# Attention and gated projection on one core: score blocks of two heads in one scheduled operation, bfloat16 sums over partitions, and new planner numbers

## The chip, the cores and the metric

The kernel runs on one core of one Trainium2 chip. The metric is device time in microseconds (us), the median of the timed runs. In rows, PE is TensorE's matmul, PEld its weight load, DVE is VectorE, ACT is ScalarE, POOL is GpSimd, and SP is the engine whose queue issues the transfers.

## The reference

Causal attention for 4 batches of 12 heads, 448 tokens, head dimension 64, in float32; then its output, as 1792 tokens by 768, goes through a gated product and two projections:

```
scores = scale * q @ k.T;  masked above the diagonal;  attn = softmax(scores)
x   = (attn @ v), heads side by side          # 1792 x 768
a   = x @ w1;  b = x @ w2                     # 768 -> 1024
out = ((a * b) @ w3) @ w_out                  # 1024 -> 1024 -> 768
```

## The kernel before

**Arithmetic.** Large products run on float16 halves: an operand is scaled by a power of two and split into a high and a low float16, and three matmuls (high·high, high·low, low·high) add up in one PSUM bank. The scale comes from a root of the sum of squares: ScalarE squares a tile and sums each row (`squares`), TensorE adds the row sums over all 128 partitions with one matmul by a matrix of ones (`root_scale`, float32, one column), and three small VectorE operations make the power of two and its inverse. The two last weights are multiplied ahead, w3·w_out, in float32 (`w34_mm`, line 738), so that each batch needs a gate (lines 862 to 864) and one projection (lines 922 to 924).

**Attention.** A "pair" is two heads; there are 6 pairs in a batch and 24 in all. Its score blocks are numbered u: 0 to 2 are head one's row blocks of 128, 256 and 384 causal columns, 3 to 5 the same of head two, and 6 is the last 64 rows of both heads together, 448 wide. Head one lies on partitions 0 to 63 and head two on 64 to 127, so the contraction is 64 rows high and the two heads use two halves of the array ("row" below; block 6 uses two quarters, "quad"; the products with v use column halves, "col"). In batches 0 and 1 q and k are float32 (`turned_whole`, each matmul is two records in the trace); in batches 2 and 3 they are float16 halves (`halved`, three matmuls to a block, each one record), and each of q and k has its own `root_scale`. Each block leases one PSUM bank, TensorE writes it (line 535), VectorE scales, masks, takes the row maximum (line 548), ScalarE takes the exponential and its row sum (line 552). `inverse` makes the reciprocals (lines 559, 562), once for blocks 0 to 5 and once for block 6. `soft` makes the float16 halves (lines 577 to 584), a transposing transfer turns them, and `values` multiplies by v (lines 605, 610) into the single "av" bank, which lines 619 and 622 empty into `xt`.

**PSUM.** Eight banks: mm 2, sc 4, tr 1, av 1. The first three row blocks of w3·w_out (`nf=3`, two banks each) hold both mm banks, three of the four sc banks and av while they accumulate over eight steps.

**Order.** Nothing is ordered by hand. Every operation is registered with a due time, its engines with a cost for each, and its reads and writes (`prog.add`). `Program.order` plays a list schedule in Python: on each engine the available operation with the least due time goes first, a bank is leased when the first operation that uses it starts, and instructions are emitted in that order. Due times come from the numbers in `PLAN`. `flex` and `pflex` are added to the due time of an operation that could run on several engines when VectorE or GpSimd considers it. Before, each head's block (and in batches 2 and 3 each of its three products) is an operation of its own that can be parted from its partner by other work.

Of the kernel before, what the change touches and what calls it, by code (L numbers as in the profile page):

```python
# [12 lines left out]
F32 = mybir.dt.float32  # L13
# [13 lines left out]
PLAN = dict(nc=10, wstep=1.7166, soft=35.104, w0=98.515, w34=0.4939, ab=1.864, out=0.1056, gap=7.934, lat=54.674, begin=124.998, wlead=108.279, urgent=16.283, flex=130.436, sc=-28.657, vo=40.18, av=-169.824, x=-3.797, qlead=-32.59, rlead=35.586, v0=19.144, v1=119.702, gram=2, nf=3, h0=3, hv=5, ns=7, wo0=-202.976, wo1=85.211, wom=33.979, w3a=4.552, w3l=33.088, wd=8.804, wh=-51.436, wl=37.619, fin=-41.134, ev=24.84, po=[-24.82, -29.77, -25.56, 9.87, -19.33, -0.94, -43.34, -41.67, -23.49, 5.24, -22.89, 3.16, 5.14, -57.04, -27.78, -11.26, -24.23, -9.57, -25.8, -22.59, -36.97, -12.49, -9.7, 9.83], wo=[-14.34, 44.19, 8.45, 71.74, 57.42, 19.24, 47.18, 16.79], w3=[-59.5, -58.87, -85.5, 5.22, 4.06, -19.4, -19.39, -66.35], tw=[-46.97, -85.5, -45.39, -9.91, -31.02, -57.6, -51.35, -51.53, -46.68, -51.96, -96.47, -10.29, -68.89, -30.15, -61.14, 9.88], slack=0.7, pflex=74.578, fq=2, hlead=23.223)  # L27
# [6 lines left out]
}  # L34

# [11 lines left out]
class Program:  # L47
# [3 lines left out]
    def __init__(self):  # L51
        self.ops, self.writer, self.readers = [], {}, {}
        self.banks, self.leased, self.first = {}, [], set()
# [5 lines left out]
    def add(self, due, how, reads=(), writes=(), stage=None):  # L59
# [17 lines left out]
        self.ops.append((round(due + 3.7e-5, 3), how, deps, stage))  # L77
        leases = [k for k in list(reads) + list(writes) if isinstance(k, Lease)]
        self.leased.append(leases[0] if leases else None)
        if leases:  # L80
            if not leases[0].users:
                self.first.add(i)
            leases[0].users += 1
        return i

    def order(self):
# [12 lines left out]
        dma_free = 0.0  # L99
# [11 lines left out]
        while len(result) < n:  # L111
# [22 lines left out]
            lease = self.leased[i]  # L134
            if i in self.first:
                found = [(at, n_, k) for k in lease.pools for at, n_ in banks[k]]
                if not found:
                    waiting.append(i)
                    continue
                at, n_, k = min(found)  # L140
                if at > t:
                    ready_at[i] = at
                    push(i)
                    continue
                banks[k].remove((at, n_))
                lease.bank, lease.home = self.banks[k][n_], (k, n_)
# [7 lines left out]
            else:  # L154
                if e == DVE and cost > 0.4:
                    cost += 0.4 * max(0.0, min(free[POOL], t + cost) - t)
                if e == PE and cost:
                    if t - free[PE] > 3.4 or not free[PE]:
# [6 lines left out]
            if lease is not None:  # L165
# [36 lines left out]
def tile_causal_attention_moe(ctx: ExitStack, tc: tile.TileContext, q, k, v, w1, w2, w3, wo, out):  # L202
# [47 lines left out]
    ones32 = cst.tile([P, P], F32, name="ones32")  # L250
    diag = cst.tile([P, P], BF16, name="diag")
    nc.vector.memset(ones, 1.0)
    nc.vector.memset(ones32, 1.0)
# [104 lines left out]
    def root_scale(sums, keys, name, due, keep=None):  # L358


        e, ek = keep or small(1, f"{name}_e")
        s, sk = small(1, f"{name}_s")
        ps, pk = prog.lease("sc", "tr")

        def total():
            for j, am in enumerate(sums):
                nc.tensor.matmul(ps[:, 0:1], ones32, am, start=j == 0, stop=j == len(sums) - 1)

        prog.add(due, (PE, 0.05 + 0.15 * len(sums), total), keys, [pk])
        prog.add(due, (DVE, 0.1, lambda: nc.vector.tensor_scalar(  # L370
            out=e.bitcast(I32), in0=ps[:, 0:1].bitcast(I32), scalar1=1, scalar2=0x7F800000,
# [3 lines left out]
        prog.add(due, (DVE, 0.09, lambda: nc.vector.reciprocal(out=s, in_=e)), [ek], [sk])  # L375
        return s, sk, e, ek

    def scaled(dst, src, s, n, due, reads, writes, view=None):
# [7 lines left out]
        ], reads, writes)  # L386

    def remainder(dst, src, s, hi, n, due, reads, writes, stage=None):

        prog.add(due, (DVE, t_dve(n) + 0.06, lambda: nc.vector.scalar_tensor_tensor(  # L390
            out=dst, in0=src, scalar=s, in1=hi, op0=ALU.mult, op1=ALU.subtract)), reads, writes, stage)
# [67 lines left out]
    def halved(p, b, hs, T, qk, qkk, qt, qtk):  # L459

        q16 = qt.rearrange("p i f -> p (i f)").bitcast(F16).rearrange("p (i t f) -> p i t f", i=2, t=2)
        inverse_of = []
        for i, src in ((1, k), (0, q)):
# [9 lines left out]
            am, ak = small(1, "qam")  # L473
            squares(am, flat, lambda n16=n16: n16[:, 1].bitcast(BF16), 4 * P, T - PLAN["hlead"], raw_k, [ak, nk])
            sc_, sck, e, ek = root_scale([am], [ak], "q", T - PLAN["hlead"])
            inverse_of.append((e, ek))
            scaled(n16[:, 0], flat, sc_, 4 * P, T - PLAN["hlead"] + 0.5, raw_k + [sck], [nk])
            remainder(n16[:, 1], flat, sc_, n16[:, 0], 4 * P, T - PLAN["hlead"] + 1, raw_k + [sck, nk], [nk])
# [3 lines left out]
        (ek_, kk), (eq_, kq) = inverse_of  # L482
        prog.add(T, (DVE, 0.1, lambda: nc.vector.tensor_scalar(  # L483
            out=iv, in0=ek_, scalar1=eq_, scalar2=-SCALE, op0=ALU.mult, op1=ALU.mult)), [kk, kq], [ivk])
# [8 lines left out]
    def pair(p):  # L493
# [28 lines left out]
        def scores(u, due):  # L522
            i, c, w, lo = place(u)
            ps, key = prog.lease("sc")
            (t32, tk) = heads[i]
            o = t32[:, lo : lo + w]
            m = mask_t if i == 2 else mask[:, (2 - c) * P :]

            n = min(P, S - c * P)

            def products(qs, ks, start, stop):
                for j in range(2):
                    rows = slice(j * D, (j + 1) * D)
                    if i in (2, j):
                        nc.tensor.matmul(ps[rows if i == 2 else slice(0, P), :w], qs[rows, c * P : c * P + n], ks[rows, 0:w],  # L535
                                         start=start, stop=stop)

            if halves:
                q16 = qt.rearrange("p i f -> p (i f)").bitcast(F16).rearrange("p (i t f) -> p i t f", i=2, t=2)
                for m_, (a, b_) in enumerate(((0, 0), (0, 1), (1, 0))):  # L540
                    prog.add(due + 0.01 * m_, (PE, t_mm(w) / (1 if i == 2 else 2) + 0.02, lambda a=a, b_=b_, m_=m_: products(
                        q16[:, 0, a], q16[:, 1, b_], m_ == 0, m_ == 2)),
                        [qtk + (1,), qtk + (0,)], [key, tk + (c,)] + ([tk] if p < 2 else []))
            else:
                prog.add(due, (PE, 0.9 if i == 2 else max(2 * t_mm(w) + 0.1, 0.31), lambda: products(
                    qt[:, 0], qt[:, 1], True, True)),
                    [qtk + (1,), qtk + (0,)], [key, tk + (c,)] + ([tk] if p < 2 else []))
            prog.add(due + 0.4, (DVE, t_dve(w) + 0.09, lambda: nc.vector.tensor_tensor_reduce(  # L548
                out=o, in0=ps[:, :w], in1=m, scale=iv, scalar=-NEG,
                op0=ALU.add, op1=ALU.min, accum_out=mx[:, u : u + 1])),  # L550
                [key, ivk, "mask_t" if i == 2 else "mask"], [mk + (u,), tk + (c,)] + ([tk] if p < 2 else []))
            prog.add(due + 0.9, (ACT, t_act(w, pointers=1, acc=True), lambda: nc.scalar.activation(  # L552
                out=o, in_=o, func=AF.Exp, scale=-1.0, bias=mx[:, u : u + 1], accum_out=sm[:, u : u + 1])),
                [mk + (u,)], [tk + (c,), smk + (u,)])
# [9 lines left out]
        def soft(i, us, due):  # L564
# [3 lines left out]
            for u in reversed(us):  # L568
# [5 lines left out]
                else:  # L574
# [8 lines left out]
                ], [tk + (c,), rck + (u,), dk], [dk + (c, 0)])  # L583
                prog.add(due + 0.4, (DVE, t_dve(w) + 0.06, lambda src=src, r=r, h=h, l=l: nc.vector.scalar_tensor_tensor(  # L584
                    out=l, in0=src, scalar=r, in1=h, op0=ALU.mult, op1=ALU.subtract)),
                    [tk + (c,), rck + (u,), dk + (c, 0)], [dk + (c, 1)])
# [14 lines left out]
        def values():  # L601
# [5 lines left out]
            for a in range(3):  # L607
                for n, (tv, tp) in enumerate(((0, 0), (1, 0), (0, 1))):
# [6 lines left out]
                 [t[1] for t in turned] + [v2k + (0,), v2k + (1,)], [ok])  # L615
# [14 lines left out]
    def decode(raw, rawk, n, due, t=None, tk=None):  # L630
# [4 lines left out]
        if t is None:  # L635
            t, tk = a, [ak]
        low = ("low", rawk[0])
        prog.add(due, (ACT, t_act(n), lambda: nc.scalar.activation(
            out=a, in_=raw[:, :, 1].bitcast(F32), func=AF.Copy, scale=2.0**-112)), rawk, [ak])
        prog.add(due, (ACT, t_act(n), lambda: nc.scalar.activation(  # L640
            out=raw[:, :, 0], in_=raw[:, :, 0].bitcast(U32), func=AF.Copy, scale=2.0**-29)), rawk, [low])
        prog.add(due + 1, (DVE, t_dve(n, True), lambda: nc.vector.tensor_scalar(
            out=ai, in0=ai, scalar1=3, scalar2=None, op0=ALU.logical_shift_left)), [ak], [ak])
        prog.add(due + 1, (DVE, t_dve(n) + 0.06, lambda: nc.vector.scalar_tensor_tensor(
            out=raw[:, :, 0], in0=raw[:, :, 1], scalar=-0x80000000, in1=raw[:, :, 0], op0=ALU.bitwise_and, op1=ALU.bitwise_or)),
            rawk + [low], [low])
# [18 lines left out]
    def take_w(i):  # L665
# [18 lines left out]
        ], tk + [sk] + w5, [("w16h", i)])  # L684
        prog.add(T + PLAN["wl"], (DVE, t_dve(DM) + 0.06, lambda: nc.vector.scalar_tensor_tensor(
            out=w16[i][:, 1], in0=tc2, scalar=s, in1=w16[i][:, 0], op0=ALU.mult, op1=ALU.subtract)),
            tk + [sk, ("w16h", i)] + w5, [("w16l", i)])
# [335 lines left out]
```

## Time and profile before

| | |
|---|---|
| median of 3 runs | 618.22 us (615.7 to 618.64) |
| span of the profiled execution | 614.8 us; its time outside the span is not listed |
| mean granted TensorE clock | 0.979 of full speed |
| busy share of the span | PE 94%, DVE 69%, ACT 55%, POOL 34% |

A record of a matmul lasts until its result has drained, so records overlap. The distance from one record's start to the next one's start is the time that a matmul holds the array, and it is this distance that the text adds up.

### The profile page before, as it was taken

The numbers are of one execution on the slowest core, as the hardware profiler recorded it, in microseconds if no ns is written. First come the engines' busy times: TensorE is split into PE (matmuls) and PEld (weight loads), VectorE is DVE, ScalarE is ACT, GpSimd is POOL, SyncE is SP. The second block draws the span as 40 slices with busy tenths as digits, with TensorE's granted clock in tenths as the row PEclk, the third lists the DMA queues.
The fourth block names the chain that finished last, engine by engine and source line by source line (L and its number), as shares of the span: only waits on it lengthen the run. The fifth ranks groups of instructions, "written<-read, shape, count | busy, mean of one in ns | idle before, by whom it ended". The sixth has DMA issues, their size and how long they took to land.

```text
span 614.8 us, 11067 instructions
## 1 busy us (share of the span) xinstructions
PE 579.4 (94%) x3940; PEld 328.6 (53%) x3940; DVE 422.5 (69%) x1135; ACT 335.6 (55%) x795; POOL 206.9 (34%) x144
## 2 busy tenths in 40 slices
PE   2899879999699999999999999999999999999997
PEld 1454445555355555555655555555555556555564
DVE  6976988999889979888158877963698970222100
ACT  7537877887567767776255655443556641111111
POOL 5651577554744536431004422300144520000000
PEclk9999988999689999999999999999999999999999
DMA  8799696564679979887934894887187863000011
GB/s 336 256 254 218 137 239 165 157 182 143 120 152 177 193 136 169 140 147 146 193 59 95 142 157 94 175 165 177 43 142 140 126 129 83 14 1 1 1 51 52
DMA packets 224951, 84.62 MB, mean 138 GB/s; under 512 B 205952, under 2 KB 221824, under 8 KB 224896
## 3 DMA queue, kind: packets, MB, share of 16 engines
q1 hardware_dynamic: 224896, 83.91, 63.9%
q8 instruction: 31, 0.51, 0.4%
q14 instruction: 24, 0.20, 0.1%
HBM read 43.78 MB, written 5.51 MB: 80 GB/s over the span
## 4 chain that ended last, share of the span: by engine, by line
PE 63%; DMA 3%; DVE 2%; ACT 2%; issue 1%; POOL 1%; SPq 0%; ACTq 0%; POOLq 0%; DVEq 0%
PE mm L862 8%; PE mm L863 7%; PE mm L864 7%; PE sc L535 6%; PE mm L922 4%; PE mm L924 4%; PE mm L923 4%; PE tr L862 3%; PE tr L863 3%; PE tr L864 3%; PE av L610 3%; PE tr L922 2%; PE tr L924 2%; PE tr L923 2%; DMA pt<-ph 2%; PE av L605 2%
## 5 line engine op out<-in xcount | busy, mean ns | idle before, releaser
L862 PE MATMUL mm<-xt,w 128*128 128x448 f16 x270 | 95.9, 355 | 0.0
L863 PE MATMUL mm<-xt,w 128*128 128x448 f16 x270 | 95.4, 353 | 0.3 <-DVE xt L622 0.3
L864 PE MATMUL mm<-xt,w 128*128 128x448 f16 x270 | 95.5, 354 | 0.0
L552 ACT ACTIVATE p<-p,mx 128x384 f32<-128x384 f32 (+2 forms) x144 | 71.7, 499 | 30.6 <-DVE mx L548 27.3
L535 PE MATMUL sc<-qkt 64*128 64x128 f16 (+6 forms) x480 | 80.5, 366 | 1.6 <-DVE mx L548 1.6
L738 PE MATMUL mm<-wof,w3t 128*128 128x384 f32 x192 | 74.9, 521 | 2.7 <-POOL wof L647 2.6
L584 DVE SCALAR_TENSOR_TENSOR ph<-p,rc,ph 128x384 f16<-128x384 f32 (+2 forms) x144 | 76.4, 577 | 1.4 <-POOL ph L581 0.7
L581 POOL TENSOR_SCALAR ph<-p,rc 128x256 f16<-128x256 f32 (+2 forms) x41 | 46.7, 1144 | 58.2 <-DVE rc L562 17.1
L862 PEld LDWEIGHTS <-w 128*128 128x128 f16 x384 | 39.4, 102 | 36.0 <-issue 5.0
L864 PEld LDWEIGHTS <-w 128*128 128x128 f16 x384 | 37.5, 98 | 35.9 <-issue 1.0
L863 PEld LDWEIGHTS <-w 128*128 128x128 f16 x384 | 37.6, 98 | 29.0 <-issue 0.2
L384 POOL TENSOR_SCALAR v<-vr,v_s 128x512 f16<-128x512 f32 x19 | 33.6, 1768 | 52.8 <-PE av L610 39.7
L384 POOL TENSOR_SCALAR da<-qkr,q_s 128x512 f16<-128x512 f32 x10 | 15.9, 1592 | 105.2 <-DVE qiv L483 97.5
L922 PE MATMUL mm<-w34h,arena 128*128 128x384 f16 x152 | 49.8, 327 | 0.0
L924 PE MATMUL mm<-w34h,arena 128*128 128x384 f16 x152 | 49.6, 327 | 0.0
L923 PE MATMUL mm<-w34l,arena 128*128 128x384 f16 x152 | 49.6, 326 | 0.0
L738 PEld LDWEIGHTS mm<-wof,w3t 128*128 128x128 f32 x192 | 35.4, 199 | 23.8 <-POOL wof L647 4.1
L862 PE MATMUL tr<-xt,w 128*128 128x448 f16 x114 | 40.3, 354 | 0.0
L864 PE MATMUL tr<-xt,w 128*128 128x448 f16 x114 | 40.2, 353 | 0.0
L863 PE MATMUL tr<-xt,w 128*128 128x448 f16 x114 | 40.2, 353 | 0.0
L548 DVE CUSTOM_DVE_ANT_0 p<-sc,mask,qiv 128x384 f32<-128x384 f32 (+2 forms) x72 | 31.0, 480 | 10.7 <-PE sc L535 10.5
L548 DVE CUSTOM_DVE_ANT_0 p<-sc,mask,minus 128x384 f32<-128x384 f32 (+2 forms) x72 | 32.7, 476 | 7.3 <-PE sc L535 7.3
(183 smaller groups left out, 1150.2 us busy)
## 6 DMA issues: line engine op xcount, KB each, us to landing
arena<-in_moe_w_dram SPq DMA_DIRECT2D x11, 768.0 KB, 5.0
vr<-in_v_dram SPq DMA_DIRECT2D x24, 192.0 KB, 3.7
out_dram<-osb SPq DMA_DIRECT2D x24, 192.0 KB, 2.1
arena<-in_moe_w_dram SPq DMA_DIRECT2D x8, 512.0 KB, 4.9
xt<-in_moe_w_dram SPq DMA_DIRECT2D x5, 768.0 KB, 6.5
qkr<-in_k_dram SPq DMA_DIRECT2D x12, 224.0 KB, 5.6
qkr<-in_q_dram SPq DMA_DIRECT2D x12, 224.0 KB, 6.3
arena<-in_moe_w_out_dram SPq DMA_DIRECT2D x3, 768.0 KB, 6.9
```

The source lines that it names most:

```text
L384: (POOL, t_pool(n) + 0.35e-3 * n + 0.16, lambda: nc.gpsimd.tensor_scalar(out=dst, in0=src, scalar1=s, scalar2=None, op0=ALU.mult)),
L535: nc.tensor.matmul(ps[rows if i == 2 else slice(0, P), :w], qs[rows, c * P : c * P + n], ks[rows, 0:w], start=start, stop=stop)
L548: prog.add(due + 0.4, (DVE, t_dve(w) + 0.09, lambda: nc.vector.tensor_tensor_reduce(out=o, in0=ps[:, :w], in1=m, scale=iv, scalar=-NEG, op ...
L552: prog.add(due + 0.9, (ACT, t_act(w, pointers=1, acc=True), lambda: nc.scalar.activation(out=o, in_=o, func=AF.Exp, scale=-1.0, bias=mx[:, ...
L584: prog.add(due + 0.4, (DVE, t_dve(w) + 0.06, lambda src=src, r=r, h=h, l=l: nc.vector.scalar_tensor_tensor(out=l, in0=src, scalar=r, in1=h ...
L738: prog.add(due, (PE, 4 * t_mm(NH), lambda: nc.tensor.matmul(ps[:, :NH], w3t[slot(m)][:, g], wof[:, g, ns], start=g == 0, stop=g == KF - 1) ...
L862: nc.tensor.matmul(ps[:, :S], w[:, 0, d], xh, start=d == 0, stop=False)
L863: nc.tensor.matmul(ps[:, :S], w[:, 0, d], xl, start=False, stop=False)
L864: nc.tensor.matmul(ps[:, :S], w[:, 1, d], xh, start=False, stop=d == KD - 1)
L922: nc.tensor.matmul(t, gh[:, fc, cs], w34h[:, fc, ns], start=fc == 0, stop=False)
L923: nc.tensor.matmul(t, gh[:, fc, cs], w34l[:, fc, ns], start=False, stop=False)
L924: nc.tensor.matmul(t, gl[:, fc, cs], w34h[:, fc, ns], start=False, stop=fc == KF - 1)
```

## The change

- The blocks of both heads with the same rows, (2,5), (1,4) and (0,3), become one operation each, which leases two sc banks and emits the heads' matmuls alternately; block 6 stays alone. They come in the order (2,5), (1,4), (6), (0,3).
- `inverse` runs once for all seven blocks.
- `root_scale` multiplies by bfloat16 ones, takes the high 16 bits of each float32 row sum as its operand, and sums n columns at once. In `halved` q and k share one `root_scale` with n=2 and one tile `qam`.
- The planner can lease several banks for an operation, counts 0.095 us (`SWITCH`) at each change between the array's modes, counts VectorE's slowdown beside GpSimd only for operations marked `port`, and has a few costs changed.
- All numbers in `PLAN` except `nc`, `gram`, `nf`, `h0`, `hv`, `ns` and `fq` are new.

```diff
-PLAN = dict(nc=10, wstep=1.7166, soft=35.104, w0=98.515, w34=0.4939, ab=1.864, ...
+PLAN = dict(nc=10, wstep=-0.4943, soft=151.2671, w0=97.4914, w34=0.3079, ab=3.3616, ...
+SWITCH = 0.095
...
-    def root_scale(sums, keys, name, due, keep=None):
+    def root_scale(parts, keys, name, due, keep=None, n=1):
...
-                nc.tensor.matmul(ps[:, 0:1], ones32, am, start=j == 0, stop=j == len(sums) - 1)
+                top = am.bitcast(BF16).rearrange("p (n t) -> p n t", t=2)[:, :, 1]
+                nc.tensor.matmul(ps[:, 0:n], ones, top, start=j == 0, stop=j == len(parts) - 1)
...
-            sc_, sck, e, ek = root_scale([am], [ak], "q", T - PLAN["hlead"])
+        sc_, sck, e, ek = root_scale([am], [ak + (0,), ak + (1,)], "q", T - PLAN["hlead"], n=2)
...
-        def scores(u, due):
+        def scores(us, due):
-            ps, key = prog.lease("sc")
+            banks = [prog.lease("sc") for _ in us]
...
+            prog.add(due, (PE, (3 if halves else 4) * t_mm(w) + 0.02, both), [qtk + (1,), qtk + (0,)],
+                     [key for _, key in banks] + ..., mode="quad" if i == 2 else "row")
...
-        for n, u in enumerate((2, 5, 1, 4, 0, 3, 6)):
-            scores(u, T + PLAN["sc"] + 0.3 * (2 * (n // 2) if halves else n) + 0.001 * n)
-        inverse(range(6), T + PLAN["soft"])
-        inverse(range(6, 7), T + PLAN["soft"] + 1.0)
+        for n, us in enumerate(((2, 5), (1, 4), (6,), (0, 3))):
+            scores(us, T + PLAN["sc"] + 0.6 * n)
+        inverse(range(7), T + PLAN["soft"])
```

## Rows read from the trace of the kernel before

**Rows 1.** The page: busy time, and the span in 40 slices.
```profile
PE 579.4 (94%) x3940; PEld 328.6 (53%) x3940; DVE 422.5 (69%) x1135; ACT 335.6 (55%) x795; POOL 206.9 (34%) x144
...
PE   2899879999699999999999999999999999999997
...
PEclk9999988999689999999999999999999999999999
```

**Rows 2.** Windows by granted clock: stretch, length, then busy time per engine.
```profile
8.00:87.00 79.00, 68.56 (x250) 38.29 (x250) 67.41 (x117) 52.68 (x107) 42.31 (x26) 1.00 0.93 234
87.00:97.20 10.20, 9.72 (x20) 5.57 (x21) 9.21 (x18) 9.20 (x21) 10.20 (x8) 0.50 0.51 147
97.20:158.70 61.50, 56.13 (x248) 33.04 (x247) 57.62 (x122) 49.74 (x92) 32.00 (x17) 1.00 0.67 178
158.70:172.30 13.60, 11.14 (x68) 6.85 (x68) 12.00 (x30) 7.25 (x22) 11.97 (x6) 0.50 0.34 67
172.30:230.00 57.70, 53.53 (x472) 32.49 (x470) 51.01 (x157) 41.02 (x106) 25.55 (x19) 1.00 0.92 171
230.00:510.00 280.00, 279.79 (x2269) 156.12 (x2267) 208.28 (x657) 155.46 (x417) 81.11 (x60) 1.00 0.73 137
510.00:610.00 100.00, 100.00 (x618) 56.17 (x617) 13.45 (x29) 15.70 (x28) 0.00 (x0) 1.00 0.07 23
```

**Rows 3.** Waits of PE: who waited for whom, us in total, times, longest.
```profile
PE tr L726 <- POOL arena L647: 9.4, 2, 8.2
...
PE av L605 <- DMA ptt<-pht: 5.0, 3, 3.3
```

**Rows 4.** Timeline of PE around a root sum and two score runs in batch 2: start, length.
```profile
279.10 0.28 PE L367 MATMUL sc<-qam,ones 128*128 128x1 f32 x2
279.24 0.32 PE L922 MATMUL mm<-w34h,arena 128*128 128x384 f16 x1
...
280.05 0.33 PE L924 MATMUL mm<-w34h,arena 128*128 128x384 f16 x1
280.31 0.99 PE L535 MATMUL sc<-qkt 64*128 64x384 f16 x12
281.23 0.34 PE L922 MATMUL mm<-w34h,arena 128*128 128x384 f16 x1
...
282.31 0.34 PE L535 MATMUL sc<-qkt 64*128 64x128 f16 x3
282.58 0.34 PE L922 MATMUL mm<-w34h,arena 128*128 128x384 f16 x1
```

**Rows 5.** Timeline of PE: one head's three float32 blocks.
```profile
206.13 0.35 PE L864 MATMUL mm<-xt,w 128*128 128x448 f16 x1
206.41 1.56 PE L535 MATMUL sc<-qkt 64*128 64x384 f32 x6
207.90 0.36 PE L862 MATMUL tr<-xt,w 128*128 128x448 f16 x1
```

**Rows 6.** VectorE by form: line, names, shape, count; busy us, mean ns.
```profile
L559 DVE TENSOR_SCALAR rc<-sm 128x1 f32<-128x1 f32 x24 | 3.4, 141 | 0.1
L562 DVE RECIPROCAL rc<-rc 128x1 f32<-128x1 f32 x24 | 3.6, 151 | 0.1
L373 DVE TENSOR_SCALAR q_e<-q_e 128x1 f32<-128x1 f32 x24 | 3.3, 146 | 0.2
```

**Rows 7.** Timeline of PE: first score block of pair 0.
```profile
46.20 0.91 PE L535 MATMUL sc<-qkt 64*128 64x384 f32 x2
```

**Rows 8.** Instructions by tile wof: ns min/median/max, first and last start.
```profile
L738 PE MATMUL sc<-wof,w3t x48: 486/487/848, 19.6 to 82.5; 128*128 128x384 f32 x48
...
L647 POOL TENSOR_TENSOR wof<-da,arena x3: 1847/1848/2090, 26.2 to 41.5; 128x768 int32<-128x768 int32 x3
```

**Rows 9.** VectorE's score operation, and its accumulator reads.
```profile
L548 DVE CUSTOM_DVE_ANT_0 p<-sc,mask,minus 128x384 f32<-128x384 f32 (+2 forms) x72 | 32.7, 476 | 7.3 <-PE sc L535 7.3
L548 DVE DVE_READ_ACCUMULATOR2_ANT mx<- 128x1 f32 x168 | 13.8, 82 | 0.0
```

More of the change, by code (lines that the diff above doesn't have):

```diff
@@ L51, in __init__ @@
     def __init__(self):
-        self.ops, self.writer, self.readers = [], {}, {}
-        self.banks, self.leased, self.first = {}, [], set()
+        self.ops, self.writer, self.readers, self.modes, self.port = [], {}, {}, {}, set()
+        self.banks, self.leased, self.first = {}, [], {}
     def lease(self, *pools):
@@ L57, in lease, with add @@
         return l, l
-    def add(self, due, how, reads=(), writes=(), stage=None):
+    def add(self, due, how, reads=(), writes=(), stage=None, mode=None, port=False):
         how = how if isinstance(how, list) else [how]
@@ L77, in add @@
         self.ops.append((round(due + 3.7e-5, 3), how, deps, stage))
+        if mode:
+            self.modes[i] = mode
+        if port:
+            self.port.add(i)
         leases = [k for k in list(reads) + list(writes) if isinstance(k, Lease)]
[L79 to L83, printed above, removed]
+        self.leased.append(leases)
+        fresh = [l for l in leases if not l.users]
+        if fresh:
+            self.first[i] = fresh
+        for l in leases:
+            l.users += 1
         return i
@@ L98, in order @@
         ran = [None] * n
-        dma_free = 0.0
+        dma_free, last_mode = 0.0, "full"
         banks = {k: [(0.0, n_) for n_ in range(len(v))] for k, v in self.banks.items()}
@@ L133, in order @@
                 _, i = heapq.heappop(soon[e])
[L134 to L144, printed above, removed]
+            taken = []
+            for lease in self.first.get(i, ()):
+                found = [(at, n_, k) for k in lease.pools for at, n_ in banks[k] if (at, n_, k) not in taken]
+                if found:
+                    taken.append(min(found))
+            if len(taken) < len(self.first.get(i, ())):
+                waiting.append(i)
+                continue
+            if taken and max(taken)[0] > t:
+                ready_at[i] = max(taken)[0]
+                push(i)
+                continue
+            for lease, (at, n_, k) in zip(self.first.get(i, ()), taken):
                 banks[k].remove((at, n_))
@@ L154, in order @@
             else:
-                if e == DVE and cost > 0.4:
+                if e == DVE and cost > 0.25 and i in self.port:
                     cost += 0.4 * max(0.0, min(free[POOL], t + cost) - t)
                 if e == PE and cost:
+                    mode = self.modes.get(i, "full")
+                    if mode != last_mode:
+                        cost += SWITCH
+                        last_mode = mode
                     if t - free[PE] > 3.4 or not free[PE]:
@@ L164, in order @@
             ran[i] = e
-            if lease is not None:
+            for lease in self.leased[i]:
                 lease.users -= 1
@@ L356, in squares @@
             out=junk(), in_=src, func=AF.Square, accum_out=dst)), reads, writes)
-    def root_scale(sums, keys, name, due, keep=None):
-        e, ek = keep or small(1, f"{name}_e")
-        s, sk = small(1, f"{name}_s")
+    def root_scale(parts, keys, name, due, keep=None, n=1):
+        e, ek = keep or small(n, f"{name}_e")
+        s, sk = small(n, f"{name}_s")
         ps, pk = prog.lease("sc", "tr")
         def total():
-            for j, am in enumerate(sums):
-                nc.tensor.matmul(ps[:, 0:1], ones32, am, start=j == 0, stop=j == len(sums) - 1)
-        prog.add(due, (PE, 0.05 + 0.15 * len(sums), total), keys, [pk])
-        prog.add(due, (DVE, 0.1, lambda: nc.vector.tensor_scalar(
-            out=e.bitcast(I32), in0=ps[:, 0:1].bitcast(I32), scalar1=1, scalar2=0x7F800000,
+            for j, am in enumerate(parts):
+                top = am.bitcast(BF16).rearrange("p (n t) -> p n t", t=2)[:, :, 1]
+                nc.tensor.matmul(ps[:, 0:n], ones, top, start=j == 0, stop=j == len(parts) - 1)
+        prog.add(due, (PE, 0.06 * len(parts), total), keys, [pk])
+        prog.add(due, (DVE, 0.07, lambda: nc.vector.tensor_scalar(
+            out=e.bitcast(I32), in0=ps[:, 0:n].bitcast(I32), scalar1=1, scalar2=0x7F800000,
             op0=ALU.logical_shift_right, op1=ALU.bitwise_and)), [pk], [ek])
@@ L461, in halved @@
         q16 = qt.rearrange("p i f -> p (i f)").bitcast(F16).rearrange("p (i t f) -> p i t f", i=2, t=2)
-        inverse_of = []
+        am, ak = small(2, "qam")
+        splits = []
         for i, src in ((1, k), (0, q)):
@@ L520, in place @@
             return (u // 3, u % 3, (u % 3 + 1) * P, OFF[u % 3]) if u < 6 else (2, 3, S, 0)
-        def scores(u, due):
-            i, c, w, lo = place(u)
-            ps, key = prog.lease("sc")
-            (t32, tk) = heads[i]
-            o = t32[:, lo : lo + w]
+        def scores(us, due):
+            i, c, w, lo = place(us[0])
+            n = min(P, S - c * P)
+            banks = [prog.lease("sc") for _ in us]
             m = mask_t if i == 2 else mask[:, (2 - c) * P :]
-            n = min(P, S - c * P)
             def products(qs, ks, start, stop):
@@ L533, in products @@
                     rows = slice(j * D, (j + 1) * D)
[L534 to L538, printed above, removed]
+                    ps = banks[j if i < 2 else 0][0]
+                    nc.tensor.matmul(ps[rows if i == 2 else slice(0, P), :w], qs[rows, c * P : c * P + n], ks[rows, 0:w],
+                                     start=start, stop=stop)
@@ L539, in scores, with both @@
+            def both():
+                if not halves:
+                    products(qt[:, 0], qt[:, 1], True, True)
+                    return
                 q16 = qt.rearrange("p i f -> p (i f)").bitcast(F16).rearrange("p (i t f) -> p i t f", i=2, t=2)
                 for m_, (a, b_) in enumerate(((0, 0), (0, 1), (1, 0))):
[L541 to L554, printed above, removed]
+                    products(q16[:, 0, a], q16[:, 1, b_], m_ == 0, m_ == 2)
@@ new lines, in scores @@
+            outs = [heads[place(u)[0]] for u in us]
+            prog.add(due, (PE, (3 if halves else 4) * t_mm(w) + 0.02, both), [qtk + (1,), qtk + (0,)],
+                     [key for _, key in banks] + [tk + (c,) for _, tk in outs] + ([tk for _, tk in outs] if p < 2 else []),
+                     mode="quad" if i == 2 else "row")
+            for u, (ps, key), (t32, tk) in zip(us, banks, outs):
+                o = t32[:, lo : lo + w]
+                prog.add(due + 0.4, (DVE, t_dve(w) + 0.07, lambda o=o, ps=ps, u=u: nc.vector.tensor_tensor_reduce(
+                    out=o, in0=ps[:, :w], in1=m, scale=iv, scalar=-NEG,
+                    op0=ALU.add, op1=ALU.min, accum_out=mx[:, u : u + 1])),
+                    [key, ivk, "mask_t" if i == 2 else "mask"], [mk + (u,), tk + (c,)] + ([tk] if p < 2 else []))
+                prog.add(due + 0.9, (ACT, t_act(w, pointers=1, acc=True), lambda o=o, u=u: nc.scalar.activation(
+                    out=o, in_=o, func=AF.Exp, scale=-1.0, bias=mx[:, u : u + 1], accum_out=sm[:, u : u + 1])),
+                    [mk + (u,)], [tk + (c,), smk + (u,)])
@@ L614, in pair @@
         prog.add(T + PLAN["av"], (PE, 1.49, values),
-                 [t[1] for t in turned] + [v2k + (0,), v2k + (1,)], [ok])
+                 [t[1] for t in turned] + [v2k + (0,), v2k + (1,)], [ok], mode="col")
         xb = xt[b % 2]
```

40 lines of the change are left out of this document (19 added, 21 removed).

## Prediction

> **What bounds the kernel now.** I read the page first. TensorE is busy for 94% of the span, VectorE for 69%, the others less, and the granted clock is at full speed but for two places [rows 1]. A busy share says little where records overlap, so I asked next for windows, cut where the clock changes [rows 2]. The reader should see two kernels in one. From 230 us to 610 PE is never idle (279.79 of 280.00, then all of 100.00), at the full 2.4 GHz, while VectorE has 208 of 280 and then 13 of 100 us to do. There every microsecond that the array is not held comes off the end, as long as the attention of the next batch stays ahead; with VectorE at 74% it has room. Before 230 us it is otherwise. From 8 us on PE is idle for 10.4, 0.5, 5.4, 2.5 and 4.2 us of the five windows, 23 in all, and in two of them, 10.2 and 13.6 us long, the granted clock is at 1.2 GHz, so that the 9.72 and 11.14 us busy there hold about 10 us more than they would. VectorE is busy for 85%, 90%, 94%, 88% and 88% of the same five. So the early part has two engines near their limit, and the waits of PE are for GpSimd's weights, and for a transposing transfer [rows 3]. That makes 33 us of idle and half-clocked array early that a better order could reach, and none late.
>
> **The change part by part, late stretch (from 230 us).** Here PE's own time counts, and its price is the distance between starts.
>
> Root sums. A float32 sum holds the array from 279.10 to 279.24, 0.14 us [rows 4]. There are 24 of q and k in batches 2 and 3; they become 12. The bfloat16 sum is one record instead of two and isn't in the trace. It can't be below zero and not above the 0.14 of two records; I take 0.06, a little under half, since the weights before it and the drain behind it stay. So 24 x 0.14 - 12 x 0.06 = 2.6 us, with ends of 1.7 and 3.4. The five other sums of this stretch give 5 x 0.08 = 0.4.
>
> Float16 scores. A run of (2,5) and (1,4) together, 12 matmuls, takes 0.92 us from 280.31 to 281.23; its columns, 6 x (384 + 256), would be 1.60 us one after another at 2.4 GHz, and half of that is 0.80. So the two heads do share the array, and 0.12 us go into starting and leaving. The entry costs 0.10 more: the matmul at 280.05 should have ended its 0.16 at 280.21, and the run starts at 280.31. A lone head's 128-column block takes 0.27 us to the next matmul, of which 0.16 are columns [rows 4]. Parted heads of that block thus cost 2 x (0.27 + 0.10), joined ones 0.37: 0.37 saved. In the timeline six of the twelve pairs part them, the first as shown, and three others part or serialize larger blocks, worth about 1.5 us by the same prices; together 3.7 us. Against it, each operation that the planner sets apart from its neighbours costs 0.2 us anew, and 12 more such places would take 2.4 back. I take 2.5, with ends of 1.3 and 3.7.
>
> For that 0.2 us the Trainium skill has a rule, in TensorEngine Tiling (Array Packing), Key Properties: changing the tiling mode drains the engine. The rows agree, with 0.10 us on entry and about as much on leaving; the rule speaks against small joined operations that are scattered among full-array matmuls, and by the row's price all 36 row blocks standing alone would leave the saving at its lower end, 1.3 us.
>
> Float32 scores. One head's three blocks take 1.49 us from 206.41 to 207.90 [rows 5]. Two records to a block and two passes to a record make 4 x 768 columns, 1.28 us; 0.21 go into starting and leaving. A second head beside it would be free, as in float16. For 12 pairs never joined that is 30.7 us of columns, always joined 15.4. The timeline has 36 such runs, the first at 46.20 and the last at 267.08. Added up at full clock and without waits inside them they hold 31.3 us, 3.9 of it starts of 0.107, so 27.4 of columns: about a fifth is joined by chance. The change saves 12.0 us of columns, and up to 2.6 of starts if fewer runs are left. Seven of the runs lie after 230 us and carry 2.4 to 2.8 of it; I take 2.6.
>
> Late sum: 3.0 + 2.5 + 2.6 = 8.1 us, ends 5.8 and 10.3.
>
> **Early part (to 230 us).** PE loses 10 us of float32 scores (12.0 and up to 2.6 of starts, less the late share) and 27 root sums at 0.08 saved, 2 us: 12 in all. VectorE loses the reciprocals of block 6, 0.141 + 0.151 us for each of 24 pairs [rows 6], 7.0 us, of which 3.5 early. The merged `inverse` waits for block 6 as well, which now comes before (0,3), so it has no later input than before. In batches 2 and 3 twelve roots less spare VectorE 36 operations of about 0.15 us [rows 6]; from 230 us on idle time covers that, so it is worth nothing, and if the cover went it would be 5 us more gain. Where two engines are near the limit and each waits for the other, the removed work of one is not all removed from the end: nothing of it is the lower bound, all of it (15.5) the upper. I take half, 6 + 2 = 8 us, since PE and VectorE are about equally full there (199 and 197 of 222 us).
>
> The new numbers of the planner move all operations, every transfer and both queues. No row prices them. From below: the 23 us of idle and 10 of half clock can come back at most. From above: the order can lose as well; I bound that by the second rival. In the sum I set it at zero, being a change of order with no row for either sign.
>
> **The sum.** 614.8 - 8.1 - 8 = 598.7 us of span. The median of the runs is 3.4 us above the profiled span, so 602.1; I say 602. With only the ends of the costs above, from 592 to 612.
>
> **Rivals.**
>
> *Late gain only.* The early part is set by VectorE and by the weights' way through three engines, and gets nothing for 12 us less of PE. For it: VectorE at 94% in the third window [rows 2]. Against it: in the fifth PE is at 93% as well. Then 614.8 - 8.1 + 3.4 = 610. About the same time (2.6 late and some 5 early less gain) comes out if joined float32 heads still run one after the other; the float16 run speaks against that [rows 4].
>
> *The new order mends the early part.* If about half of the 33 us come back on top, 602 - 16 = 586. For it: the planner now counts the 0.1 us of a mode change, which the rows show. The idle time has few causes, and the longest single wait is 8.2 us [rows 3]. Against it: VectorE's busy time in the first four windows adds up to 146 of 164 us, 89% [rows 2], and what it does there, decoding weights and the softmax of batch 0, the change leaves all but untouched.
>
> *Two banks at once (slower).* The score operations now need two free sc banks. w3·w_out holds three of four from 19.6 until about 82.5 us [rows 8], and the scores of pairs 0, 1 and half of pair 2 now slip through the one that is left, the first at 46.20 [rows 7]. If they must wait for the end of that group, VectorE's part of three pairs, 3 x 7 x (0.476 + 0.082) = 12 us [rows 9] with block 6 counted like the others, moves from a time with room into windows of 90% and more. With the late gain kept, 614.8 - 8.1 + 12 + 3.4 = 622. It decides from about 8 us moved on. For it: three of four banks. Against it: the last piece of w_out is written soon after 41.5 us [rows 8], so from then on the group lacks only array time, and an order that puts it first could free the banks well before 82.5. The Trainium skill has the same pressure as a rule, TensorEngine Tiling (Array Packing), PSUM Pressure: different row tiles write to different PSUM banks. The trace can't show its cost in the joined form.
>
> **How the numbers follow.** The forecast, 596 to 608 us, has 0.45; the mended early part, under 596, 0.27; late gain only, 608 to 614, 0.13; two banks, from 614 up, 0.15, of which 0.02 still is faster, 0.05 no change and 0.08 slower. What a measurement here can tell from no change is about 0.5%, 3.1 us: faster is below 615.1, slower above 621.3. So faster 0.87, same 0.05, slower 0.08. The range is 583 to 616: it takes in the ends of the costs, the late-only case and the middle of the mended one, and leaves out about 0.09 below and 0.10 above.
>
> **What would show it.** Right: 12 root records of q in place of 48; float32 runs whose two heads start within 0.01 us of each other; the fully busy stretch of PE, from the first gate product after batch 0 to the end, shorter by about 8 us for the same work; and the start of that stretch 5 to 10 us earlier. Wrong: PE waits on line 548 or on banks at 45 to 85 us; a third or longer stretch at half clock; idle PE after 230 us because a late emptied av bank holds up the next pair. That last one would break the premise that late array time is end time, and a new order can do it without any of the removed work coming back.

## The result, and the profile after

602.24 us against 618.21, median of four runs each; the ratio is 0.9742 (95% interval 0.9714 to 0.9769). The forecast was 602. The profiled execution spans 601.0 us, 13.8 less than before. The medians differ by 16.0. A time is about 1.8 us over its span in these runs, so the profiled execution of before lies some 1.6 us under its median, and that of after 0.5 over its own. No trace shows where these 2 us lie. The page after, busy time and the same two lines of slices:

```profile
PE 552.8 (92%) x3872; PEld 308.4 (51%) x3872; DVE 424.4 (71%) x1076; ACT 328.4 (55%) x768; POOL 195.6 (33%) x145
...
PE   2899983899778999999999999999999999999997
...
PEclk9999996799988999999999999999999999999999
```

PE is busy for 26.6 us less than in [rows 1], about twice the gain, and its share of the span has fallen. The places at lower clock have not gone: they stand in slices 7 and 8 now, and more faintly in 12 and 13.

One mark divides both kernels well: the first product of batch 0's norms, which needs the attention of all of batch 0. It is the first record that reads xt into an sc bank (first and last start):

```profile
L813 PE MATMUL sc<-xt x96: 195/219/230, 203.8 to 524.5; 128*128 128x128 f16 x72, 128*64 128x64 f16 x24
```

after the change

```profile
L827 PE MATMUL sc<-xt x96: 196/219/222, 202.7 to 516.9; 128*128 128x128 f16 x72, 128*64 128x64 f16 x24
```

Windows cut at this mark, before (columns as in [rows 2]; the last three figures of a row are the granted clock, where 1.00 is 2.4 GHz, the busy share of the DMA engines, and GB/s):

```profile
8.00:203.80 195.80, 173.91 (x868) 101.33 (x869) 176.11 (x382) 140.67 (x303) 110.34 (x65) 0.94 0.79 191
203.80:610.50 406.70, 405.46 (x3075) 227.30 (x3073) 242.89 (x744) 190.39 (x486) 92.81 (x67) 1.00 0.57 110
```

and after:

```profile
8.00:202.70 194.70, 159.90 (x847) 92.45 (x848) 173.81 (x367) 140.09 (x298) 105.10 (x64) 0.93 0.80 197
202.70:596.70 394.00, 392.83 (x3027) 215.93 (x3025) 247.12 (x701) 183.62 (x466) 86.69 (x69) 1.00 0.60 111
```

The reader should see nearly the whole gain in the second row: 406.70 to 394.00, 12.7 us, with PE full in both. In the first row PE is busy for 14.0 us less and the mark comes 1.1 us earlier; the other 12.9 turned into idle time (34.8 us against 21.9). Not all of the 14.0 is removed work: PE was busy for 20.9 us at 1.2 GHz before [rows 2] and for 17.0 after, so that some 2 us of it, as an estimate, are matmuls that no longer ran at half clock. VectorE's busy time there barely moved, 176.1 to 173.8. The windows at 1.2 GHz after the change:

```profile
93.70:114.10 20.40, 10.19 (x26) 5.82 (x27) 18.88 (x40) 14.46 (x32) 13.14 (x8) 0.50 0.53 151
168.80:172.20 3.40, 3.40 (x44) 2.68 (x46) 3.40 (x14) 2.35 (x10) 0.00 (x0) 0.51 0.81 162
185.80:189.20 3.40, 3.40 (x13) 1.60 (x13) 2.15 (x7) 1.12 (x2) 1.67 (x2) 0.50 0.50 108
```

27.2 us, against 23.8 [rows 2]; in the longest PE is busy for half the time and VectorE for 93%.

The parts themselves, in PE's timeline after: a joined float32 block pair, a sum, and a float16 run.

```profile
210.19 0.35 PE L878 MATMUL tr<-xt,w 128*128 128x448 f16 x1
210.47 1.35 PE L546 MATMUL sc<-qkt 64*128 64x384 f32 x8
211.75 0.36 PE L876 MATMUL tr<-xt,w 128*128 128x448 f16 x1
...
304.80 0.17 PE L380 MATMUL sc<-qam,ones 128*128 128x2 bf16 x1
304.82 0.35 PE L876 MATMUL mm<-xt,w 128*128 128x448 f16 x1
...
308.89 0.99 PE L546 MATMUL sc<-qkt 64*128 64x384 f16 x12
309.81 0.36 PE L876 MATMUL mm<-xt,w 128*128 128x448 f16 x1
...
311.84 0.34 PE L546 MATMUL sc<-qkt 64*128 64x128 f16 x6
312.12 0.36 PE L876 MATMUL tr<-xt,w 128*128 128x448 f16 x1
```

The eight float32 records, four of 384 and four of 256 columns, take 1.28 us for two heads; one head's three blocks took 1.49 [rows 5]. The sum holds the array for 0.02 us, not 0.14 [rows 4]. The last block of both heads takes 0.28, about as much as one head's took [rows 4]. The 0.14 was not the price of every float32 sum: right behind a score run, where nine of the 34 sums after the mark stood before the change, it held the array for 0.24:

```profile
319.37 0.38 PE L367 MATMUL tr<-qam,ones 128*128 128x1 f32 x2
319.61 0.35 PE L862 MATMUL mm<-xt,w 128*128 128x448 f16 x1
```

### The profile page after: what moved, and what is told of

Its sections match the earlier page's. It is cut to its first block, busy times and chain, and to the rows that moved or that the text cites. A ratio compares the mean times of both kernels' runs of the same rounds, so it can differ in the third digit from the quotient of the medians.

```text
span 601.0 us, 10820 instructions
## 1 busy us (share of the span) xinstructions
PE 552.8 (92%) x3872; PEld 308.4 (51%) x3872; DVE 424.4 (71%) x1076; ACT 328.4 (55%) x768; POOL 195.6 (33%) x145
## 5 line engine op out<-in xcount | busy, mean ns | idle before, releaser
L877 PE MATMUL mm<-xt,w 128*128 128x448 f16 x252 | 89.0, 353 | 3.4 <-DVE xt L636 3.4
L876 PE MATMUL mm<-xt,w 128*128 128x448 f16 x252 | 89.2, 354 | 0.0
L878 PE MATMUL mm<-xt,w 128*128 128x448 f16 x252 | 89.0, 353 | 0.0
L567 ACT ACTIVATE p<-p,mx 128x256 f32<-128x256 f32 (+1 forms) x144 | 71.5, 498 | 30.8 <-DVE mx L563 30.7
L752 PE MATMUL mm<-wof,w3t 128*128 128x384 f32 x192 | 72.1, 518 | 2.8 <-POOL wof L661 1.7
L599 DVE SCALAR_TENSOR_TENSOR ph<-p,rc,ph 128x384 f16<-128x384 f32 (+2 forms) x144 | 72.5, 551 | 1.6 <-ACT ph L594 0.8
L596 POOL TENSOR_SCALAR ph<-p,rc 128x128 f16<-128x128 f32 (+2 forms) x46 | 43.4, 951 | 88.5 <-DVE rc L577 52.7
L546 PE MATMUL sc<-qkt 64*128 64x384 f16 (+7 forms) x480 | 64.3, 363 | 3.6 <-DVE inv L383 2.1
L397 POOL TENSOR_SCALAR v<-vr,v_s 128x512 f16<-128x512 f32 x17 | 28.3, 1663 | 63.4 <-PE av L624 53.0
L876 PE MATMUL tr<-xt,w 128*128 128x448 f16 x132 | 46.9, 355 | 0.0
L878 PE MATMUL tr<-xt,w 128*128 128x448 f16 x132 | 46.7, 354 | 0.0
L877 PE MATMUL tr<-xt,w 128*128 128x448 f16 x132 | 46.7, 354 | 0.0
L902 ACT CAST arena<-g 128x448 f16<-128x448 f32 x22 | 12.4, 564 | 46.4 <-DVE g L897 46.3
L656 DVE TENSOR_SCALAR da<-da 128x768 int32<-128x768 int32 (+1 forms) x38 | 28.1, 745 | 11.5 <-ACT da L652 11.4
## 6 DMA issues: line engine op xcount, KB each, us to landing
qkr<-in_k_dram SPq DMA_DIRECT2D x12, 224.0 KB, 4.4
qkr<-in_q_dram SPq DMA_DIRECT2D x12, 224.0 KB, 5.2
```

The source lines that it names most:

```text
L596: (POOL, t_pool(w) + 0.35e-3 * w + 0.16, lambda src=src, r=r, h=h: nc.gpsimd.tensor_scalar(out=h, in0=src, scalar1=r, scalar2=None, op0=AL ...
L752: prog.add(due, (PE, 4 * t_mm(NH), lambda: nc.tensor.matmul(ps[:, :NH], w3t[slot(m)][:, g], wof[:, g, ns], start=g == 0, stop=g == KF - 1) ...
L876: nc.tensor.matmul(ps[:, :S], w[:, 0, d], xh, start=d == 0, stop=False)
L877: nc.tensor.matmul(ps[:, :S], w[:, 0, d], xl, start=False, stop=False)
L878: nc.tensor.matmul(ps[:, :S], w[:, 1, d], xh, start=False, stop=d == KD - 1)
```

## The experiments

Two theories stood at the start. W: the gain is array time of removed work, from about 200 us on. N: the gain is the new order. "Mark" below is the first norms product of batch 0 in the profiled execution, "rest" the span from there to its end. Both are of one execution each. Four kernels with the same code up to the mark (changed, heads_in_turn and the two late runs) have it between 201.6 and 203.6 us, and the four early runs, whose code behind the mark is that of the changed kernel, have rests between 396.7 and 400.6; smaller differences than these are not to be read.

| run | median us | ratio to before (interval) | mark | rest |
|---|---|---|---|---|
| before | 618.2 | | 203.8 | 411.0 |
| changed | 602.24 | 0.9742 (0.9714 to 0.9769) | 202.7 | 398.3 |
| old_numbers | 627.08 | 1.0148 (1.0120 to 1.0175) | 224.0 | 397.3 |
| new_numbers_alone | 634.71 | 1.0266 (1.0240 to 1.0291) | 214.1 | 419.3 |
| parted_old_numbers | 623.33 | 1.0109 (1.0068 to 1.0151) | 215.7 | 406.7 |
| bf16_sums_alone | 613.55 | 0.9929 (0.9908 to 0.9950) | 204.7 | 406.5 |
| f32_sums_back | 604.54 | 0.9801 (0.9775 to 0.9828) | 202.4 | 399.4 |
| heads_in_turn | 602.70 | 0.9757 (0.9731 to 0.9783) | 203.6 | 399.4 |
| early_pe_twice | 605.09 | 0.9777 (0.9747 to 0.9807) | 204.6 | 398.7 |
| late_pe_twice | 621.07 | 1.0053 (1.0034 to 1.0073) | 201.9 | 416.6 |
| early_dve_twice | 619.70 | 1.0031 (1.0010 to 1.0052) | 220.0 | 397.3 |
| late_dve_twice | 634.72 | 1.0279 (1.0250 to 1.0309) | 201.6 | 430.8 |
| early_no_low | 597.81 | 0.9665 (0.9638 to 0.9693) | 195.5 | 400.6 |
| early_half_turn | 591.94 | 0.9599 (0.9558 to 0.9640) | 193.0 | 396.7 |

**old_numbers: the changed code, the numbers of before.**

```diff
-PLAN = dict(nc=10, wstep=-0.4943, soft=151.2671, ...
+PLAN = dict(nc=10, wstep=1.7166, soft=35.104, ...
```

> The changed code with the planner numbers of before. Theory W (the gain is array time of removed work, from about 200 us on): the joined scores and short sums save the same 12 us late under any order that keeps attention ahead, so 603 to 609 us. Theory N (the gain is the new order): 614 us or more, about the time before.

**new_numbers_alone: the code of before, the new numbers** (the same line the other way).

> The code of before with the new planner numbers. Theory W: no array time is removed, so 613 to 625 us. Theory N: 600 to 606 us, most of the gain without any of the code.

Both are slower than before. For the first, W's range failed by 18 us; N's "614 us or more" holds it, but not its "about the time before". For the second both theories missed, W's 613 to 625 and N's 600 to 606. The rest of old_numbers, 397.3 us, is that of the changed kernel: the late gain needs the code and not the numbers. Its mark is 20 us late. PE's waits show where (us in total, times, longest):

```profile
PE sc L546 <- DVE mx L563: 16.8, 10, 6.6
```

These are score operations that wait for VectorE to read banks; nearly all of it lies between 107 and 220 us. In the changed kernel the same wait is 1.2 us in 4 pieces. The clock has a part too: up to the mark 47.8 us stand at 1.2 GHz, against 27.2 in the changed kernel, and PE is busy for 168.7 us there, 8.8 more, with nearly the same matmuls. So the numbers don't bring the gain, they pay off a loss of some 20 us that the new code has under the old ones. The numbers alone place the mark 10 us late and make the rest 8 us longer; PE is then busy for 411.1 us of the rest, against 405.5 before, and its float16 scores come in 40 runs there, not in 31.

**parted_old_numbers: as old_numbers, but each head's score block an operation with one bank again** (the function `scores` and its loop of before; short sums and single `inverse` stay).

```diff
-        for n, us in enumerate(((2, 5), (1, 4), (6,), (0, 3))):
-            scores(us, T + PLAN["sc"] + 0.6 * n)
+        for n, u in enumerate((2, 5, 1, 4, 0, 3, 6)):
+            scores(u, T + PLAN["sc"] + 0.3 * (2 * (n // 2) if halves else n) + 0.001 * n)
```

> The changed code with the numbers of before, but each head's score block is again an operation of its own with one bank (short sums and single reciprocal stay). Theory B (with the old numbers the joined operation waits for two banks and holds TensorE in the first 200 us): the waits of line 546 on the maxima fall from 32 us to a few, the norms of batch 0 come at 203 to 210 us instead of 224, and the stretch from there to the last product is 4 to 6 us longer than the 392.8 of joined blocks: 608 to 614 us. Rival O (the old numbers fit no other code, whatever is changed): the norms of batch 0 stay at 215 us or later, 620 us or more.

The wait on VectorE's maxima falls to 1.6 us, and the mark comes 8.3 us earlier, at 215.7, not the 14 or more of theory B: the two banks are under half of the loss in these two executions, and the rest of it stays with numbers that were made for another list of operations, as rival O had it. The profiled execution of old_numbers was its fastest, 3.9 us under its median, so the 8.3 can be up to 12. The rest of the span grows by 9.4 us. The sums are short in both, but not all of that is the scores: added up by the distances between starts, the row runs hold 27.3 us behind the mark, against 21.6 when joined, 5.7 more; the other 3.7 stand in other operations.

**bf16_sums_alone: the kernel before in its own order, with short sums.**

```diff
-nc.tensor.matmul(ps[:, 0:1], ones32, am, start=..., stop=...)
+nc.tensor.matmul(ps[:, 0:1], ones, am.bitcast(BF16)[:, 1:2], start=..., stop=...)
```

> The kernel before in its own order, only the sums over partitions by bfloat16 ones and the high halves (planner costs unchanged, so nothing moves). Theory W with the sum's price as the traces now show it (34 sums from 200 us on, 7.5 us held before; 22 sums hold 0.65 after, 0.03 each): 6 us faster, 611 to 613. As the prediction priced it (0.08 a sum): 2.5 us faster, 615 to 616.5. Rival: the weights' load before a sum stands in the way all the same, no change, 617 to 619.

4.5 us against the runs of the kernel before beside it, and 4.5 in the rest: more than the forecast's price, less than the 6 that was expected before the run. 34 sums lie there, so 0.13 each, near the difference between the 0.14 and the 0.02 shown above. Before the mark the run says something else:

```profile
8.00:204.70 196.70, 169.29 (x845) 96.04 (x845) 175.57 (x382) 140.32 (x303) 109.72 (x65) 0.94 0.78 190
```

PE is busy for 4.6 us less there than before (173.91), and the mark comes no earlier. The sums that were shortened early gave nothing in the order of before.

**f32_sums_back: the changed kernel in its own order, with float32 sums** (the same edit reversed, q and k still merged).

> The changed kernel in its own order, with the sums over partitions again by float32 ones and float32 row sums (q and k still in one sum). 22 sums lie after 200 us. If a float32 sum costs 0.13 us more (4.5 us over 34 sums, as the run of before with bfloat16 sums gave): 605 us. If the prediction's 0.08: 604. If it is the merging of q and k and not the type that saves: 602.

2.3 us by the medians, near the 2.9 of 22 x 0.13, and 3.6 by the two ratios to the kernel before. So the type counts, but the run can't tell 0.13 from 0.08 a sum. The 1.1 in the rest is within its spread.

**heads_in_turn: head one's three float16 products before head two's** (in block 6 too).

```diff
...
-                for m_, (a, b_) in enumerate(((0, 0), (0, 1), (1, 0))):
-                    products(q16[:, 0, a], q16[:, 1, b_], m_ == 0, m_ == 2)
+                for j in range(2):
+                    for m_, (a, b_) in enumerate(((0, 0), (0, 1), (1, 0))):
+                        products(q16[:, 0, a], q16[:, 1, b_], m_ == 0, m_ == 2, (j,))
```

> The changed kernel in its own order, but in batches 2 and 3 the three products of head one are emitted before the three of head two, for the row blocks; block 6 too. Theory W: per pair two more streams of 160 + 107 + 53 + 187 ns hold the array, 12 x 1.0 = 12 us, all of it at the end: 612 to 616 us. Rival (the array lets head two start while head one streams, whatever the order of emission): 601 to 604.

The rival holds. The run of twelve still takes 0.92 us:

```profile
310.86 0.99 PE L546 MATMUL sc<-qkt 64*128 64x384 f16 x12
311.78 0.36 PE L877 MATMUL mm<-xt,w 128*128 128x448 f16 x1
```

So it is not that heads alternate that makes them share the array, but that nothing else stands between them.

**early_pe_twice: float32 score products of batch 0 done twice.**

```diff
-                    products(qt[:, 0], qt[:, 1], True, True)
+                    for _ in range(2 if b == 0 else 1):
+                        products(qt[:, 0], qt[:, 1], True, True)
```

> The changed kernel in its own order, with every float32 score matmul of batch 0 done twice: 6 x (1.28 + 0.75) = 12 us more array time, all before 200 us. If the early part takes half of what the array saves there, as predicted: 608 us. If PE does not set the early part: 600 to 604. If the longer busy array keeps the clock up: under 602.

**late_pe_twice: float16 score products of batches 2 and 3 done twice** (the same loop, in the other branch).

> The same with every float16 score matmul of batches 2 and 3 twice: 12 x (3 x 0.320 + 3 x 0.187) = 18 us more array time, after 300 us. Theory W: it all comes out at the end, 618 to 622 us. Rival (the late part has room, for instance behind the norms of each batch): under 612.

12 us of array time early cost 2.9 us, between the two expectations (the mark moves by 1.9, no more than its spread); 18 us late cost 18.8. That is the premise of the forecast for the late stretch, measured, and at most a sixth to a quarter, not a half, for the early one.

**early_dve_twice: VectorE's remainder of the attention weights twice in batch 0**, and **late_dve_twice**, the same in batches 2 and 3.

```diff
...
-nc.vector.scalar_tensor_tensor(out=l, in0=src, scalar=r, in1=h, op0=ALU.mult, op1=ALU.subtract)
+[nc.vector.scalar_tensor_tensor(out=l, in0=src, scalar=r, in1=h, op0=ALU.mult, op1=ALU.subtract)
+ for _ in range(2 if b == 0 else 1)]
...
```

> The changed kernel in its own order, with VectorE's remainder of the attention weights done twice in batch 0: 42 operations, 6 x 4.2 = 25 us more VectorE work, between about 60 and 195 us. If VectorE's load sets the early part: 617 to 627 us. If it is a chain of hops between engines or the transfers with slack on VectorE: 602 to 610.

> The changed kernel in its own order, with VectorE's remainder of the attention weights done twice in batches 2 and 3: 84 operations, 12 x 4.2 = 50 us more VectorE work between 310 and 510 us. If VectorE has room late, as the premise of the prediction says: 601 to 605 us. If it is near its limit there too: over 615.

VectorE's busy time up to the mark grows by 22.2 us, not by the 25 expected, and 17.5 come out at the end, all before the mark: more work for VectorE early is paid for. Not all of that is waiting for VectorE: 44.4 us of the stretch stand at 1.2 GHz, against 27.2, and PE is busy for 6.3 us longer with the same matmuls. Late, its busy time grows by 43.4 us, not by 50, and 32.5 come out, a miss: VectorE's room late covers about a quarter of that. Its windows, early_dve_twice up to the mark:

```profile
8.00:220.00 212.00, 166.20 (x847) 94.67 (x848) 196.05 (x409) 140.43 (x298) 103.28 (x64) 0.90 0.75 181
```

and late_dve_twice from the mark on:

```profile
201.60:628.20 426.60, 405.21 (x3027) 219.96 (x3025) 290.53 (x785) 183.34 (x466) 85.73 (x69) 0.97 0.53 103
```

The second row has PE idle for 21.4 us, where the changed kernel has 1.2, and PE is busy for 12.4 us longer with the same matmuls, at a mean clock of 0.97. The two make up the 32.5.

**early_no_low: no remainder in batch 0** (`range(0 if b == 0 else 1)` in the same place; the buffers are cleared as a whole at the start).

> The changed kernel without VectorE's remainder of the attention weights in batch 0 (left out: the low half of the weights there, which stays zero; the buffers are cleared once as a whole). 25 us less VectorE work before 195 us. If VectorE sets the early part: 582 to 594 us. If the transfers, GpSimd's weights or a chain set it: 597 to 602.

```profile
8.00:195.50 187.50, 155.00 (x848) 89.42 (x849) 156.24 (x327) 140.86 (x301) 103.69 (x64) 0.94 0.84 203
```

VectorE's busy time falls by 17.6 us, to 156, not by the 25 expected. The mark comes 7.2 us earlier, of which 4.4 are left at the end, and 597.81 lies in the second expectation's range. Adding to VectorE costs nearly eight tenths of what its busy time grows by, taking away gives four tenths back at the mark and a quarter at the end: below its present load something else is close.

**early_half_turn: as before, and the low half is neither turned nor multiplied in batch 0** (half the bytes of its 18 turning transfers).

> The run without VectorE's remainder in batch 0, and now the low half of the weights isn't turned or multiplied there either (left out: the low half of batch 0's weights): the 18 turning transfers of batch 0 move half the bytes, TensorE's products with v fall by a third there. If, once VectorE is lighter, the transfers hold the early part, the norms of batch 0 come before 191 us instead of at 195.5, and 590 to 594 us. If something else holds it (the weights through three engines, the scores, the engines' hops): 194 to 196 and 596 to 598 us.

The mark comes at 193.0, between the two expectations, and the rest is 3.9 us shorter than in early_no_low, which neither had and which is the whole spread of the rests. Whether transfers hold the early part next is not settled by it: the values' products got shorter as well.

## Why the forecast came out

The total was right by luck; its division was not. Two errors of the sum, 8.1 late and 8 early against 12.7 and 1.1, cancelled but for 2.3 us of span (598.7 forecast, 601.0 measured). Those were covered by a third: the sum put 3.4 us between span and median, and after the change it is 1.2. The forecast divided at 230 us and the measurement at the mark; by the forecast's own prices that moves some 1 us from early to late.

**Premise.** That array time from 230 us on is end time held: 18 us added there cost 18.8. VectorE's reserve behind it is smaller than "74% busy" suggested (late_dve_twice), but the change didn't use it up.

**Root sums, late: 3.0 forecast, 4.5 measured for the type alone** (bf16_sums_alone), **6 to 7 for type and merge together.** By the distances between starts, the sums held PE for 7.5 us behind the mark, 1.0 of it a wait, and hold it for 0.65 after the change. The term was mis-sized, and it is the larger error of the late sum. 0.06 for the new sum was a guess between bounds; it is 0.03 on average, near the lower one. The 0.14 for the old sum was one row's, and nine sums behind score runs held 0.24. And counted from the mark the late stretch holds 34 float32 sums, not the 29 after 230 us. The Trainium skill puts about 60 cycles on a matmul, however few its columns (TensorEngine Tiling (Array Packing), Instruction Overhead); at 2.4 GHz that is 0.025 us as an estimate. The new sums agree with it, with 0.02 in the row of 304.80 and 0.65 for all 22.

**Joined scores, late: 5.1 forecast, 5.3 by the same distances.** Behind the mark the float32 row runs hold PE for 7.3 us instead of 9.6, 2.3 where 2.6 were forecast, and the float16 row runs for 15.0 instead of 18.0, 3.0 where 2.5 were forecast. Sums and row runs make up 12.2 of the 12.7 us. So mechanism and size were right. The experiments alone bound this term from above: 12.7 less 4.5 still has the merge of the sums in it, and parted against joined under the old numbers, 9.4, has other work in it. The forecast let the planner scatter joined blocks and took back 1.2 us for it. It kept them close: 24 float16 runs after, 31 before, and 123 changes of mode after 200 us against 146.

**Early part: 8 forecast, 1.1 measured.** This is the step that failed: "I take half, since PE and VectorE are about equally full there". PE lost about the 12 us of work that I had counted (14.0 of busy time, some 2 of it the clock), and it was worth next to nothing; 1.1 is within the spread of the mark. In bf16_sums_alone, too, 4.6 us less of busy PE brought the mark no earlier. Prices as measured since: at most a sixth to a quarter of what PE is given, four tenths of what is taken from VectorE. The same fullness in a window doesn't make two engines equal. That VectorE's work stands in a chain and PE's fills its gaps would explain it, and is not shown. PE's freed time turned into idle time, and the longest stretch at 1.2 GHz grew from 13.6 us to 20.4 in a place where PE is busy half the time. Whether that longer stretch itself cost time wasn't tried.

**VectorE's removed operations.** 7.0 us less was the forecast for `inverse`. By the view of groups its two lines took 9.6 + 7.8 = 17.4 us before, and 6.1 + 4.8 = 10.9 after, 6.5 less. The operations of one column [rows 6] are gone. Of the others the reciprocal is longer for its seventh column (200 ns against 185), the other line is not (253 against 271). VectorE's busy time up to the mark fell by 2.3 us, where 3.5 were forecast; at the price above that is under 1 us of time.

**New numbers, set at zero.** For the pair of kernels that was right, mark 203.8 and 202.7, and for a reason I had not seen. With the code of before they cost 2.7%, and without them the new code is slower than before by 1.5%. So zero is not a price of theirs: they and the code were only good together.

**Rivals.** *Late gain only* was the truth in kind, with 12.7 us late in place of its 8.1. *The mended early part* did not happen: idle and half-clocked time there grew. *Two banks at once* exists: under the old numbers it is 8.3 us of the mark's delay, up to 12 by the medians (12 were the price), but not where I put it (46 to 83 us): the waits come at 107 us and later. In the changed kernel the order leaves 1.2 us of that wait. Beside it I had set a rule of the Trainium skill, that different row tiles write to different PSUM banks (TensorEngine Tiling (Array Packing), PSUM Pressure). The traces agree that this is a pressure here: 16.8 us of waits in that run, 1.6 with one bank to an operation.

What stays open: what costs old_numbers its remaining 12 us, and what is next behind VectorE in the early part. Among the candidates for the first are the planner's own changes (`SWITCH`, `port` and the new costs), which no run took out of the new code.

## What to carry to other kernels

Find a mark that divides a kernel where its limit changes, and price an edit on each side by adding work as well as by removing it: 18 us of matmuls cost 18.8 us on one side and 12 us cost 2.9 on the other. Take the added load from the trace, not from the plan: 50 us of VectorE work planned were 43 in its busy time. Where an order is planned by search, code and numbers are one thing; a part tried alone under the other's numbers shows its cost in a stretch that is bound by its own work, not in the total. Price an operation by all its places: a float32 sum held the array for 0.14 us among full-array matmuls and for 0.24 right behind a score run. In these runs two row halves of the array share it as long as nothing stands between their matmuls, and every lone visit costs 0.2 us.

## What was unexpected of the hardware

Matmuls of one array half don't wait for those of the other that were issued earlier: with head one's three products issued before head two's, records still start in pairs 0.010 us apart (0.003 when issued alternately), and the run takes 0.92 us either way. And a one-record bfloat16 sum between full matmuls holds the array for 0.02 to 0.03 us, a float32 one of one column for 0.14, and for 0.24 right behind a score run.
